# Positions of the global attention steps, and the order of the last output blocks, in a fused attention and two-MLP kernel

## Chip, cores and metric

The kernel runs on one core of one Trainium2 chip. The metric is the device time of one execution in microseconds (us); lower is better. The core's engines are PE (TensorE matmul; PEld is its weight load), DVE (VectorE), ACT (ScalarE), POOL (GpSimd) and SP (SyncE, which here only issues DMAs; SPq and ACTq are the DMA issues of SP and of ACT).

## What is computed

Attention over 32 global and 512 local positions (4 batches, 8 heads of 64), then two blocks on the 4 x 576 x 512 result, everything in float32:

```python
s_g = scale * q_g @ k_all.T                   # global rows see everything
out_g = sm(s_g) @ v_all
s_ll = where(|i - j| <= 32, scale * q_l @ k_l.T, -1e9)
s_l = concat([scale * q_l @ k_g.T, s_ll])     # local rows: a band and the globals
out_l = sm(s_l) @ concat([v_g, v_l])
x = concat([out_g, out_l]) as (4, 576, 512)
xn = (x - mean) / sqrt(var + 1e-6) * g_ln
x = x + relu(xn @ w_ch1) @ w_ch2              # first block, 512 -> 2048 -> 512
h = relu(x @ w_in)                            # second block, 512 -> 1024
conv = 3-tap convolution of h along the sequence
out = (h * sigmoid(conv)) @ w_out             # 1024 -> 512
```

## The kernel before

**Work units.** Most matmuls take a float32 operand as a high and a low part, so one product is three matmuls. Attention is cut into 64 local steps n = 0 to 63 (batch n // 16, tile t of 128 rows = n // 4 % 4, head pair hp = n % 4) and 16 global steps (one per batch and head pair). `GAT` (L37) says before which local step each global step stands; the list `order` is built from it. Rows of attention output are gathered into 17 tiles (16 local ones and one, "g", that holds all global rows), and the tiles into 8 chunks of 3, 2, 2, ... tiles. The first block (L825 hidden product, L849, L850 and L854 output product) runs chunk by chunk, in 16 units per chunk, while the attention of later chunks is mixed in: a pacing function (`tick`) hands out the small pieces of the steps so that, from a quarter of a chunk ahead of chunk k to a quarter ahead of chunk k + 1, the steps that chunk k + 1 needs are issued evenly (for k from 4 on, chunks counted from 0). A scheduler then fixes the order of each engine's instructions.

**Steps and their round trip.** A local step computes scores (L342, L343 on PE), adds the mask and takes the row limits (L346, DVE), and takes exponentials (L355, ACT). From n = 22 on the transposition of these goes through DRAM, for two steps (an even one and the odd one behind it, called pair 52/53 and so on) together: each step turns 32 x 32 blocks on DVE (L377) and stores them (`leave`, L381 on SP), and after the odd one four DMAs read both back in transposed order (`arrive`, L390 on SP). Then PE multiplies with the values, both steps behind each other (L416 for inner tiles, L409 to L411 for edge tiles t = 0 and 3). A global step has two halves of scores (L474, L475), a transpose on PE (L496) and its values (L505). L568 transposes a finished tile for the first block.

```python
for i, s in enumerate(order):
    s.out = i + 1
    if s.far and s.hp % 2:
        s.mate = [t for t in order[:i] if isinstance(t, Local)][-1]
        s.out = s.mate.out = i + LAG          # LAG = 3
```

So the values of a pair are issued three places in `order` behind its odd step, whatever stands in these places. SP issues its DMAs in order, among them the loads of later steps: `raw` (L298, L445, waits for POOL's split of the step whose buffer it takes), `rawv` (L303), `rawg` (L453), and the stores of finished tiles (`yscr`, L806).

**The end.** In the second block, `output(b, f)` (L1204) multiplies hidden block f of batch b with its 128 rows of `w_out`: for each of the four row tiles t three matmuls (L1192 to L1194) into that tile's own bank. Behind f = 7 each tile is copied to one of four buffers `osb` (`emit`, L1198) and stored. The rows of the 32 leading positions of all four batches lie together in `grem`, written by POOL (L1134, L1135), and make one product of 24 matmuls, `orem`. PE keeps program order in the whole second block. At the end come blocks 4, 5 and 6 of batch 3 (`steps[-4:-1]`), `orem` with four stores (L1252), then block 7 with the copies of its four tiles, by ACT and DVE in turn, the last tile in two halves of 256 columns (L1215, L1216).

Of the kernel before, what the change touches and what calls it, by code (L numbers as in the profile page):

```python
# [17 lines left out]
P = 128  # L18
B, H, SL, SG, D = 4, 8, 512, 32, 64
S = SL + SG  # L20
DM = H * D
FF, F2 = 2048, 1024
NF, NF2, NDC = FF // P, F2 // P, DM // P
NT = SL // P
# [9 lines left out]
BIG = 3.0e38  # L34

CHUNKS = [3, 2, 2, 2, 2, 2, 2, 2]
GAT = [24, 26, 28, 30, 32, 34, 36, 38, 40, 42, 44, 46, 49, 52, 53, 54]  # L37

WARM0 = 13
B_ATT = 300  # L40
# [32 lines left out]
def tile_kernel(ctx: ExitStack, tc: tile.TileContext, a_w, a_x, a_e, a_m, g_qk, g_v, w12, g_ln, w_in, w_out, conv_w, out):  # L73
    nc = tc.nc
    PE, DVE, ACT, POOL, SP = nc.tensor, nc.vector, nc.scalar, nc.gpsimd, nc.sync
# [24 lines left out]
    def keep_order(at, engines, to=None):  # L100

        last = {}
        for ins in traced()[at:to]:
            if ins.engine in engines:
                if ins.engine in last:
                    tc.add_manual_dep(ins, last[ins.engine].name, mybir.DependencyInfo(
                        mybir.DependencyClass.NoSync, mybir.DependencyReason.DATA), reason="order")
                last[ins.engine] = ins

    def copy(e, dst, src):  # L110
        if e is ACT:
            ACT.activation(dst, src, AF.Copy)  # L112
        else:
            e.tensor_copy(dst, src)

    def split(hi, lo, src, e_hi, e_lo):

        copy(e_hi, hi, src)
        return e_lo.tensor_tensor(lo, src, f32(hi), op=ALU.subtract)  # L119
# [25 lines left out]
    def w_stages(i, tag, fps, e_lo):  # L145

        n = 2 * DM // len(fps)
        cols = [slice(k * n, (k + 1) * n) for k in range(len(fps))]
        ops = []

        def start():
            raw = wraw.pop(i)
            for c, fp in zip(cols, fps):
                fp = fp()
                ops.append((fp, narrow(fp, raw[:, c], fp)))
                with behind("act"):
                    ops[-1][1][0]()

        def hi():
            w = wpool.tile([P, 2, 2 * DM], F32R, tag=f"w{tag}", name="w")  # L160
            wt[i] = w[:, 0], w[:, 1]
            for c, (fp, _) in zip(cols, ops):
                ACT.activation(w[:, 0, c], fp, AF.Copy)  # L163

        def lo():
            for c, (fp, _) in zip(cols, ops):
                e_lo.tensor_tensor(wt[i][1][:, c], fp, f32(wt[i][0][:, c]), op=ALU.subtract)

        def middle(k):
            for _, o in ops:  # L170
                o[k]()

        return [start], [lambda k=k: middle(k) for k in (1, 2)], [hi, lo]
# [80 lines left out]
    def next_qs(n):  # L254

        if n >= SPARE and spare:
            places[:] = spare
            spare.clear()
        places.append(places.pop(0))
        return places[-1]  # L260

    def score_bank(n):

        return (ps_t, "t") if n < SHARE else (ps_a, "s")
# [166 lines left out]
    class Global:  # L431
# [23 lines left out]
        def split(self):  # L455
            self.qs = next_qs(GAT[self.b * NP + self.hp])
            self.kh = apool.tile([P, S], F32R, tag="kh", name="kh", bufs=2)
# [8 lines left out]
        def half(self, i):  # L466
            ks = slice(i * self.HALF, (i + 1) * self.HALF)
            pool, tag = score_bank(GAT[self.b * NP + self.hp])
            ps = pool.tile([P, self.HALF], F32, tag=tag, name="ps")
# [57 lines left out]
    for n in range(B * NT * NP):  # L527
        b, t, hp = n // NP // NT, n // NP % NT, n % NP
        order += [Global(g // NP, g % NP) for g in range(B * NP) if GAT[g] == n]
        order.append(Local(b, t, hp, n))  # L530
        if hp == NP - 1:
            tiles.append((b, t))
            if n - NP < GAT[-1] <= n:
                tiles.append("g")
# [503 lines left out]
    for p in range(NPR):  # L1038
        st = w_stages(("o", p), p, [lambda k=k: mpool.tile([P, 2 * DM], F32, tag=f"fpx{k}", name="fpo")[:, :DM]
                                    for k in range(2)], DVE)  # L1040
# [68 lines left out]
    osbs = wpool.tile([P, 4, DM], F32, tag="w4", name="osb")  # L1109
    gts, ops = {}, {}  # L1110
# [27 lines left out]
    def hidden(b, p, at):  # L1138

        a, x = wae[p], wx[p]  # L1140
        n = b * NPR + p
        he, ho = hs[2 * n % 4], hs[(2 * n + 1) % 4]
        p1s, u2, u3 = (us[:, n % 2 * 3 + i] for i in range(3))

        def add(name, o, i0, i1):
            with ahead(B_ADD):
                named[name, n] = DVE.tensor_tensor(o, i0, i1, op=ALU.add)

        px = ps_x.tile([P, HB], F32, tag="px", name="px")
        product(px, a, 0, "B11", True, "first")  # L1150
        with ahead(B_ADD):
            named["p1s", n] = ACT.activation(p1s, px, AF.Copy)
        at("B11")
        py = ps_x.tile([P, HB], F32, tag="py", name="py")
        product(py, x, 1, "T2", True, "first")
        add("u2", u2, py, p1s)
        at("T2")
        pv = ps_v.tile([P, HB], F32, tag="pv", name="pv")
        product(pv, x, 0, "T3", True)
        add("u3", u3, pv, u2)  # L1160
        at("T3")
        pz = ps_v.tile([P, HB], F32, tag="pz", name="pz")
        product(pz, a, 2, "T1", True)
        add("e1", he[:, U1], pz, u3)
        at("T1")
        at(0)

        def t4():
            product(pv, a, 3, "T4", False)
            add("e0", he[:, U0], pv, u2)  # L1170
            named["relu", n] = ACT.activation(he[:, 1:1 + S], he[:, 1:1 + S], AF.Relu)
            at("T4")

        def b21():
            product(px, a, 1, "B21", False)
            with ahead(B_ADD):
                named["relu0", n] = ACT.activation(ho[:, U0], px, AF.Relu)
            at("B21")

        for part in (b21, t4) if n < 2 else (t4, b21):  # L1180
            part()
        gate(b, 2 * p, he)
        product(pz, x, 2, "B22", False)
        add("o1", ho[:, U1], pz, u2)
        named["relu1", n] = ACT.activation(ho[:, U1], ho[:, U1], AF.Relu)
        at("B22")
        gate(b, 2 * p + 1, ho)
        at(1)

    def mm_o(o, gh, gl, f, first, last):  # L1190
        wh, wl = (w[:, f % 2 * DM:(f % 2 + 1) * DM] for w in wt["o", f // 2])
        PE.matmul(o, gh, wh, start=first, stop=False)  # L1192
        PE.matmul(o, gh, wl, start=False, stop=False)  # L1193
        PE.matmul(o, gl, wh, start=False, stop=last)  # L1194

    nout = [0]

    def emit(o, e=ACT):  # L1198
        osb = osbs[:, nout[0] % 4]
        nout[0] += 1  # L1200
        copy(e, osb, o)
        return osb

    def output(b, f):  # L1204
        gh, gl = gts.pop((b, f))
        if f == 0:
            ops[b] = [ps_o.tile([P, DM], F32, tag=f"o{t}", name="po2") for t in range(NT)]
        for t in range(NT):
            tk = slice(SG + t * P, SG + (t + 1) * P)
            mm_o(ops[b][t], gh[:, tk], gl[:, tk], f, f == 0, f == NF2 - 1)  # L1210
            if (b, f, t) == (B - 1, NF2 - 1, NT - 1):
                osb = osbs[:, nout[0] % 4]
                for c, e, q in ((0, DVE, SP), (1, ACT, ACT)):
                    cols = slice(c * DM // 2, (c + 1) * DM // 2)
                    copy(e, osb[:, cols], ops[b][t][:, cols])  # L1215
                    q.dma_start(out[b, SG + t * P:SG + (t + 1) * P, cols], osb[:, cols])  # L1216
            elif f == NF2 - 1:
                e = DVE if b == B - 1 and t % 2 else ACT
                (ACT if e is DVE else SP).dma_start(out[b, SG + t * P:SG + (t + 1) * P, :], emit(ops[b][t], e))

    steps = [(b, f) for b in range(B) for f in range(NF2)]
    second = len(traced())
# [3 lines left out]
    for i in range(B * NPR):  # L1226
        b, p = divmod(i, NPR)
# [14 lines left out]
                    named["yc", b, n] = y_split(n)  # L1242

        hidden(b, p, at)
    for st in steps[-4:-1]:
        output(*st)
    o = ps_v.tile([P, DM], F32, tag="pv", name="orem")
    for f in range(NF2):
        mm_o(o, grem_h[:, f], grem_l[:, f], f, f == 0, f == NF2 - 1)
    orem = emit(o)  # L1250
    for b in range(B):
        (ACT if b % 2 else SP).dma_start(out[b, :SG, :], orem[b * SG:(b + 1) * SG])  # L1252
    output(*steps[-1])
    keep_order(second, [mybir.EngineType.PE])
    for order in HEAD + [[("e0", NPR * b + 2), ("sum", b, 3)] for b in range(1, B - 1)] + [
            [("u3", NPR * b + 3), ("e1", NPR * b + 3), e] for b in range(1, B - 1) for e in (("yc", b, "T3"), ("mul", b, 4))]:
# [113 lines left out]
```

## Time and profile before

| | us |
|---|---|
| median of 3 runs | 722.61 |
| lowest and highest of them | 719.81, 726.59 |
| the profiled execution | 721.07 |
| span of its trace | 719.3 |

The span is from the first to the last instruction of the profiled execution; the 1.77 us between it and that execution's own time lie outside the trace. A row of the timeline starts with its start in us from the span's start and its duration; what stands in brackets behind it is the idle time of that engine before it and what ended it. The matmuls of one row overlap, so PE's pace is read from the starts of successive rows.

### The profile page before, as it was taken

What the parts mean: (1) busy time and instruction counts of PE and PEld (TensorE: products, weight loads), DVE (VectorE), ACT (ScalarE), POOL (GpSimd) and SP (SyncE); (2) the same over time, 40 slices, a digit from 0 to 9 for tenths busy, and PEclk for the clock granted to TensorE, in tenths of its full rate; (3) what the DMA queues carried; (4) which work ended last, traced back from release to release, by engine and by line L of the source; (5) the groups of instructions that cost most, each with busy time, mean ns of one, the idle gap of its engine ahead of it and who ended that gap; (6) DMA issues with size and microseconds to landing.
All of it is one profiled execution on the core that took longest, in us unless ns stands there. A gap on an engine that the chain in (4) does not pass through costs nothing.

```text
span 719.3 us, 12803 instructions
## 1 busy us (share of the span) xinstructions
PE 703.3 (98%) x4517; PEld 627.9 (87%) x4517; DVE 474.6 (66%) x1168; ACT 402.5 (56%) x961; POOL 173.5 (24%) x236
## 2 busy tenths in 40 slices
PE   9989999999999999999989999999999999999997
PEld 5778899889988999999988999998899888988985
DVE  3889973755655475556538523763988989889770
ACT  6859663565566656656645411432656766566551
POOL 1012022444455344434434200000001122201000
PEclk9999999999999999999999999999999999999999
DMA  8993224775676667567547732315510121110102
GB/s 357 424 420 110 73 93 117 179 189 153 165 196 185 171 165 193 150 186 177 150 109 177 183 78 45 102 60 153 231 52 13 63 74 16 63 59 0 60 1 73
DMA packets 120144, 98.25 MB, mean 137 GB/s; under 512 B 84128, under 2 KB 102160, under 8 KB 117520
## 3 DMA queue, kind: packets, MB, share of 16 engines
q1 hardware_dynamic: 119552, 96.73, 46.2%
q8 instruction: 35, 0.57, 0.3%
q10 hardware_dynamic: 528, 0.70, 0.3%
q14 instruction: 29, 0.24, 0.1%
HBM read 77.49 MB, written 19.92 MB: 135 GB/s over the span
## 4 chain that ended last, share of the span: by engine, by line
PE 75%; DMA 11%; DVE 6%; ACT 2%; issue 2%; SPq 2%; POOL 0%; ACTq 0%; DVEq 0%; POOLq 0%
PE ph L825 20%; PE yps L854 7%; PE yps L849 7%; PE yps L850 6%; PE po L1194 4%; PE po L1193 4%; PE po L1192 4%; PE po L416 3%; DMA wraw<-w 3%; PE pv L1121 3%; PE px L1121 3%; PE pz L1121 3%; DMA trip<-trip 3%; DMA trip<-stage 3%; PE py L1121 1%
## 5 line engine op out<-in xcount | busy, mean ns | idle before, releaser
L825 PE MATMUL ph<-xe,w 128*128 128x256 f32 (+1 forms) x768 | 116.2, 297 | 0.9 <-ACT w L163 0.9
L825 PEld LDWEIGHTS ph<-xe,w 128*128 128x128 f32 x768 | 107.8, 188 | 5.8 <-ACT w L163 1.2
L849 PE MATMUL yps<-w,hh 128*128 128x512 f32 x272 | 109.4, 402 | 0.9 <-ACT hh L834 0.4
L850 PE MATMUL yps<-w,hh 128*128 128x512 f32 x272 | 107.7, 396 | 0.0
L825 PE MATMUL ph<-xo,w 128*128 128x256 f32 x768 | 105.5, 282 | 0.0
L834 ACT ACTIVATE hh<-ph 128x256 fp32r<-128x256 f32 (+1 forms) x128 | 50.4, 394 | 97.6 <-PE ph L825 86.0
L825 PEld LDWEIGHTS ph<-xo,w 128*128 128x128 f32 x768 | 99.9, 188 | 3.9
L119 POOL TENSOR_TENSOR kl<-raw,kh 128x448 fp32r<-128x448 f32 (+2 forms) x59 | 71.1, 1205 | 127.7 <-ACT kh L112 112.0
L835 DVE SCALAR_TENSOR_TENSOR hl<-ph,hh 128x256 fp32r<-128x256 f32 x112 | 46.4, 415 | 56.1 <-ACT hh L834 55.7
L854 PE MATMUL yps<-w,hl 128*128 128x512 f32 x224 | 72.5, 397 | 0.7 <-DVE hl L835 0.7
L346 DVE CUSTOM_DVE_ANT_0 sm<-ps,mask 128x192 f32<-128x192 f32 (+1 forms) x128 | 42.8, 368 | 33.9 <-PE ps L343 22.8
L355 ACT ACTIVATE sm<-sm,nm 128x192 f32<-128x192 f32 (+1 forms) x128 | 58.5, 458 | 10.1 <-DVE nm L346 9.8
L112 ACT ACTIVATE kh<-raw 128x448 fp32r<-128x448 f32 (+2 forms) x59 | 34.3, 581 | 48.1 <-PE ps L342 25.9
L849 PEld LDWEIGHTS yps<-w,hh 128*128 128x128 f32 x272 | 51.1, 188 | 8.9 <-ACT hh L834 1.4
L850 PEld LDWEIGHTS yps<-w,hh 128*128 128x128 f32 x272 | 51.2, 188 | 6.1
L1127 DVE SCALAR_TENSOR_TENSOR c<-hs,cw,c 128x544 f32<-128x544 f32 x64 | 48.9, 779 | 4.0 <-ACT c L1125 2.7
L1193 PE MATMUL po<-w,gh 128*128 128x512 f32 x128 | 50.7, 396 | 0.0
L1194 PE MATMUL po<-w,gl 128*128 128x512 f32 x128 | 50.7, 396 | 0.0
L854 PEld LDWEIGHTS yps<-w,hl 128*128 128x128 f32 x224 | 41.2, 188 | 10.8 <-DVE hl L835 1.9
L1192 PE MATMUL po<-w,gh 128*128 128x512 f32 x128 | 50.6, 395 | 0.0
L1134 POOL CAST grem<-gh 128x32 fp32r<-128x32 f32 x32 | 14.4, 450 | 120.3 <-ACT gh L112 120.3
L478 DVE CUSTOM_DVE_ANT_0 sm<-ps,tmpg 64x272 f32<-64x272 f32 x32 | 13.8, 431 | 37.2 <-ACT tmpg L477 37.2
(193 smaller groups left out, 1441.4 us busy)
## 6 DMA issues: line engine op xcount, KB each, us to landing
wraw<-w SPq DMA_DIRECT2D x16, 1024.0 KB, 17.1
trip<-trip SPq DMA_DIRECT2D x84, 128.0 KB, 3.3
raw<-a_m SPq DMA_DIRECT2D x23, 352.0 KB, 3.4
raw<-a_e SPq DMA_DIRECT2D x20, 320.0 KB, 3.3
trip<-trip SPq DMA_DIRECT2D x21, 256.0 KB, 3.7
trip<-stage SPq DMA_DIRECT2D x21, 256.0 KB, 3.2
raw<-g_qk SPq DMA_DIRECT2D x16, 304.0 KB, 3.0
rawg<-g_v SPq DMA_DIRECT2D x16, 280.0 KB, 3.5
```

The lines of the kernel that those rows point to most:

```text
L119: return e_lo.tensor_tensor(lo, src, f32(hi), op=ALU.subtract)
L355: ACT.activation(s, s, AF.Exp, bias=self.nm[:, j:j + 1], scale=-1.0, accum_out=xt.sums[:, h:h + 1])
L825: e = PE.matmul(ph[:, :n], w[:, d * P:(d + 1) * P], x[:, d], start=m == 0, stop=m == 3 * NDC - 1)
L834: ACT.activation(hh, ph[:, :n], AF.Relu)
L849: PE.matmul(yps[i], hh[:, tk], wh[:, DM:], start=edge(k, -1), stop=False)
L850: PE.matmul(yps[i], hh[:, tk], wl[:, DM:], start=False, stop=False)
L854: mark["last"] = PE.matmul(yps[i], hl[:, tk], wh[:, DM:], start=False, stop=edge(k, 1)).ins
L1121: PE.matmul(ps, wx_, y[:, d], start=start and d + m == 0, stop=d + m == 3, skip_group_check=True)
L1127: named[k, b, f] = DVE.scalar_tensor_tensor(c, h[:, k:S + k], cw[:, 3 * f + k:3 * f + k + 1], c, op0=ALU.mult, op1=ALU.add)
L1192: PE.matmul(o, gh, wh, start=first, stop=False)
L1193: PE.matmul(o, gh, wl, start=False, stop=False)
L1194: PE.matmul(o, gl, wh, start=False, stop=last)
```

## The change

It moves the global steps that stood in front of local steps 49, 52, 53 and 54 to stand in front of 48, 50, 52 and 54. At the end, `output` takes several hidden blocks at once: blocks 4 and 5 as before, then `orem` and its stores, then blocks 6 and 7 together, tile by tile (six matmuls for one tile, its copy, its store). All copies are ACT's; the last tile is copied whole and stored as two halves of 64 rows, one on SP's queue and one on ACT's.

```diff
-GAT = [24, 26, 28, 30, 32, 34, 36, 38, 40, 42, 44, 46, 49, 52, 53, 54]
+GAT = [24, 26, 28, 30, 32, 34, 36, 38, 40, 42, 44, 46, 48, 50, 52, 54]
...
-    def output(b, f):
-        gh, gl = gts.pop((b, f))
-        if f == 0:
+    def output(b, *fs):
+        pairs = [gts.pop((b, f)) for f in fs]
+        if fs[0] == 0:
             ops[b] = [ps_o.tile([P, DM], F32, tag=f"o{t}", name="po2") for t in range(NT)]
         for t in range(NT):
             tk = slice(SG + t * P, SG + (t + 1) * P)
-            mm_o(ops[b][t], gh[:, tk], gl[:, tk], f, f == 0, f == NF2 - 1)
-            if (b, f, t) == (B - 1, NF2 - 1, NT - 1):
-                osb = osbs[:, nout[0] % 4]
-                for c, e, q in ((0, DVE, SP), (1, ACT, ACT)):
-                    cols = slice(c * DM // 2, (c + 1) * DM // 2)
-                    copy(e, osb[:, cols], ops[b][t][:, cols])
-                    q.dma_start(out[b, SG + t * P:SG + (t + 1) * P, cols], osb[:, cols])
-            elif f == NF2 - 1:
-                e = DVE if b == B - 1 and t % 2 else ACT
-                (ACT if e is DVE else SP).dma_start(out[b, SG + t * P:SG + (t + 1) * P, :], emit(ops[b][t], e))
+            for f, (gh, gl) in zip(fs, pairs):
+                mm_o(ops[b][t], gh[:, tk], gl[:, tk], f, f == 0, f == NF2 - 1)
+            if fs[-1] == NF2 - 1:
+                rows, osb = out[b, tk], emit(ops[b][t])
+                if (b, t) == (B - 1, NT - 1):
+                    ACT.dma_start(rows[D:], osb[D:])
+                    rows, osb = rows[:D], osb[:D]
+                SP.dma_start(rows, osb)
...
-    for st in steps[-4:-1]:
+    for st in steps[-4:-2]:
         output(*st)
...
-    output(*steps[-1])
+    output(B - 1, NF2 - 2, NF2 - 1)
```

PE's order around the values of pair 52/53 (L416, the `x8`), before. L505 and L496 are a global step's, L474 and L475 its scores, L849 to L854 and L825 the first block's:

```order
L854 MATMUL yps<-w,hl 128x512 x2
L505 MATMUL pog<-v,ptsb 128x256 x5
L568 MATMUL ptx<-ident,xn 128x128 x4
L849 MATMUL yps<-w,hh 128x512
L850 MATMUL yps<-w,hh 128x512
L849 MATMUL yps<-w,hh 128x512
L850 MATMUL yps<-w,hh 128x512
L854 MATMUL yps<-w,hl 128x512 x2
L416 MATMUL po<-rawv,trip 128x64 x8
L474 MATMUL ps<-kh,xe 128x272
L475 MATMUL ps<-kl,xe 128x272
L825 MATMUL ph<-xe,w 128x256 x24
```

And the same values in the changed kernel, with the scores of steps 54 (first) and 55 (L342, L343):

```order
L342 MATMUL ps<-kh,xe 128x224
L343 MATMUL ps<-kl,xe 128x224
L342 MATMUL ps<-kh,xe 128x224
L343 MATMUL ps<-kl,xe 128x224
L825 MATMUL ph<-xe,w 128x256 x12
L416 MATMUL po<-rawv,trip 128x64 x5
L496 MATMUL ptg<-ident,sm 109x128 x5
L342 MATMUL ps<-kh,xe 128x224
L343 MATMUL ps<-kl,xe 128x224
L342 MATMUL ps<-kh,xe 128x224
L343 MATMUL ps<-kl,xe 128x224
L416 MATMUL po<-rawv,trip 128x64 x3
```

Before, the values stood ahead of the second half of the last global step (L474) and of the scores of step 54; now they stand behind step 54's scores and 12 more matmuls of L825.

ACT's last instructions, before (`po_8022` to `po_8025` are the banks of tiles 0 to 3 of batch 3; `DMA` is an issue on ACT's queue):

```order
L112 ACTIVATE osb<-orem 128x512
L112 ACTIVATE osb<-po_8022 128x512
L1252 DMA out<-osb 32x512 x2
L1219 DMA out<-osb 128x512
L112 ACTIVATE osb<-po_8024 128x512
L112 ACTIVATE osb<-po_8025 128x256
L1216 DMA out<-osb 128x256
```

And in the changed kernel:

```order
L112 ACTIVATE osb<-orem 128x512
L1250 DMA out<-osb 32x512 x2
L112 ACTIVATE osb<-po_8022 128x512
L112 ACTIVATE osb<-po_8023 128x512
L112 ACTIVATE osb<-po_8024 128x512
L112 ACTIVATE osb<-po_8025 128x512
L1215 DMA out<-osb 64x512
```

ACT now copies all four tiles whole, and its queue holds only two stores of `orem` and the lower half of the last tile.

SP's last issues, before:

```order
L1004 DMA yT<-yscr 128x4x544
L1219 DMA out<-osb 128x512 x8
L1252 DMA out<-osb 32x512 x2
L1219 DMA out<-osb 128x512
L1216 DMA out<-osb 128x256
L1219 DMA out<-osb 128x512
```

And in the changed kernel:

```order
L1004 DMA yT<-yscr 128x4x544
L1217 DMA out<-osb 128x512 x8
L1250 DMA out<-osb 32x512 x2
L1217 DMA out<-osb 128x512 x3
L1217 DMA out<-osb 64x512
```

Before, tile 2's store (the last row) stood behind the store of tile 3's first half; now the tiles' stores stand in their order, and the last is half a tile.

## Rows read from the trace of the kernel before

**Rows 1.** Page, part 1: engine, busy us (share of span), instructions.

```profile
PE 703.3 (98%) x4517; PEld 627.9 (87%) x4517; DVE 474.6 (66%) x1168; ACT 402.5 (56%) x961; POOL 173.5 (24%) x236
```

**Rows 2.** Windows: stretch, its length, then busy us (instructions) of PE, PEld, DVE, ACT, POOL; clock, DMA share, GB/s.

```profile
200.00:250.00 50.00, 48.12 (x332) 43.75 (x331) 28.32 (x103) 32.76 (x92) 25.56 (x25) 1.00 0.69 179
...
350.00:400.00 50.00, 47.31 (x329) 43.27 (x328) 30.43 (x99) 27.73 (x80) 20.97 (x22) 1.00 0.57 142
...
694.00:719.30 25.30, 20.26 (x91) 16.25 (x89) 7.50 (x11) 7.34 (x13) 1.28 (x4) 0.94 0.15 52
```

**Rows 3.** Waits of PE from 60 to 425 us: total us, times, longest.

```profile
PE po L416 <- DMA trip<-trip: 3.1, 3, 2.2
PE po L409 <- DMA trip<-trip: 1.3, 1, 1.3
```

**Rows 4.** Timeline of PE, 355 to 395 us: scores of 53, its values; scores of 55, its values.

```profile
356.58 0.37 PE L342 MATMUL ps<-kh,xe 128*128 128x224 f32 x1
...
365.52 0.63 PE L854 MATMUL yps<-w,hl 128*128 128x512 f32 x2
368.30 2.08 PE L416 MATMUL po<-rawv,trip 128*128 128x64 f32 x16 [2.15 <-DMA trip<-trip]
...
377.17 0.27 PE L342 MATMUL ps<-kh,xe 128*128 128x224 f32 x1
...
390.08 0.66 PE L416 MATMUL po<-rawv,trip 128*128 128x64 f32 x4 [0.52 <-DMA trip<-trip]
```

**Rows 5.** Timeline of SP: `leave` of 53, `arrive` of 52/53.

```profile
359.92 0.38 SPq L381 DMA_DIRECT2D trip<-stage  x1
363.56 1.92 SPq L390 DMA_DIRECT2D trip<-trip  x4
```

**Rows 6.** Chain that ended last, one piece of L825: start, us, what.

```profile
370.69 2.84 PE ph L825 x24
```

**Rows 7.** Timeline of PE: scores of 33 and values of 32/33; scores of 43 and values of 42/43.

```profile
198.75 0.25 PE L342 MATMUL ps<-kh,xe 128*128 128x192 f32 x1
...
211.79 0.50 PE L409 MATMUL po<-rawv,trip 128*128 128x128 f32 x2 [1.29 <-DMA trip<-trip]
...
273.88 0.35 PE L342 MATMUL ps<-kh,xe 128*128 128x224 f32 x1
...
286.29 1.76 PE L416 MATMUL po<-rawv,trip 128*128 128x64 f32 x14
```

**Rows 8.** Timeline of the end, all engines.

```profile
701.74 0.21 POOL L1135 CAST grem<-gl 128x32 fp32r<-128x32 f32 x1
...
703.06 0.39 PE L1192 MATMUL po<-w,gh 128*128 128x512 f32 x1
...
711.07 0.40 PE L1194 MATMUL orem<-w,grem 128*128 128x512 f32 x1
...
711.51 0.60 ACT L112 ACTIVATE osb<-orem 128x512 f32<-128x512 f32 x1 [10.70 <-PE orem L1194]
...
713.87 0.39 PE L1194 MATMUL po<-w,gl 128*128 128x512 f32 x1
...
714.70 0.42 DVE L114 COPY osb<-po 128x256 f32<-128x256 f32 x1 [1.10 <-ACT osb L112]
...
715.16 0.38 ACT L112 ACTIVATE osb<-po 128x256 f32<-128x256 f32 x1 [0.47 <-DVE osb L114]
715.57 0.38 ACTq L1216 DMA_DIRECT2D out<-osb  x1
715.61 0.37 SPq L1219 DMA_DIRECT2D out<-osb  x1
```

**Rows 9.** DMA issues from 714 us on: out<-in queue, count, KB each, median us to landing.

```profile
out<-osb SPq DMA_DIRECT2D x1, 256.0 KB, 2.7
out<-osb SPq DMA_DIRECT2D x1, 128.0 KB, 1.7
out<-osb ACTq DMA_DIRECT2D x1, 128.0 KB, 1.9
```

More of the change, by code (lines that the diff above doesn't have):

```diff
@@ L1196, in tile_kernel, with emit @@
     nout = [0]
-    def emit(o, e=ACT):
+    def emit(o):
         osb = osbs[:, nout[0] % 4]
         nout[0] += 1
-        copy(e, osb, o)
+        copy(ACT, osb, o)
         return osb
-    def output(b, f):
-        gh, gl = gts.pop((b, f))
-        if f == 0:
+    def output(b, *fs):
+        pairs = [gts.pop((b, f)) for f in fs]
+        if fs[0] == 0:
             ops[b] = [ps_o.tile([P, DM], F32, tag=f"o{t}", name="po2") for t in range(NT)]
```

## Prediction

> **What bounds the kernel now.** I read the page's busy times first, then windows, then PE's waits, then the timelines around them. PE is busy for 703.3 of 719.3 us [rows 1], and the change leaves the number of its matmuls as it is. So only PE's idle time (16 us in all) and what follows its last matmul can give anything. The windows say where to look: 200 to 250 us leaves PE 1.9 us idle, 350 to 400 us 2.7 us, and the end, 694 to 719.3 us, 5.0 us [rows 2]. The first of these lies ahead of everything that the change moves: PE's order differs only from local step 48 on, about 310 us into the trace. The list of waits names the cause in the middle: from 60 to 425 us PE waited 3.1 us in three times on L416 and 1.3 us once on L409, each time for the round trip of a pair's exponentials through DRAM [rows 3]. Two of these lie in reach: 2.15 us ahead of the values of pair 52/53 and 0.52 us ahead of those of 54/55, together 2.67 us [rows 4].
>
> **Why pair 52/53 waits.** Two lengths race. One is the round trip from the odd step's scores until its data are back. For 53 it is 368.30 - 356.58 = 11.7 us [rows 4], of which 3.3 pass until SP issues `leave`, 3.6 more until the first `arrive`, and the rest in the four DMAs of `arrive` [rows 5]. The other is the PE work queued between these scores and the pair's values: the last matmul ahead of the wait ends at 365.52 + 0.63 = 366.15, so 9.6 us. For 55 it is 12.9 us of round trip against 12.4 of work, for 33 it is 13.0 against 11.8 (edge values, L409), and 43 had 12.4 us of work and did not wait [rows 4, 7]. I counted the same distance for all 21 pairs in PE's order, at 0.118 us for a matmul of L825 [rows 6], 0.233 us for one with 512 columns (twelve from 711.07 to 713.87, [rows 8]) and about 0.25 us for a value matmul (a listed one is two records; 16 records take 2.08 us, [rows 4]). Three pairs come out below 11 us (22/23, 32/33 and 52/53), and all three waited; 18 have 12.0 us or more, and only 54/55 waited. So the line lies between 11 and 12 us.
>
> **Part 1, the global steps.** It removes the gap's cause: before, a global step stood between 52 and 53 and the next one right behind 53, and the values of 52/53 came ahead of step 54's scores; now two local steps lie side by side and the values come behind step 54's scores. Between 53's scores and the values stand 48 matmuls of L825 instead of 24, with 18 of 512 columns in both: 24 x 0.118 = 2.8 us more, so about 12.0 us by count and 12.3 by the trace's 9.6. The other pairs behind the point where the orders part: 46/47 12.2 us, 50/51 12.0, 54/55 12.4, 48/49 14.6, the four last over 18. None is below 11 us. 22/23 and 32/33 lie ahead of that point and keep their 0.4 and 1.3 us.
> What is late next: with a round trip of c us, the four shortest distances wait (c - 12.2) + 2 (c - 12.0) + (c - 12.4) in all. At 11.7 us, as 53 itself had, that is nothing; at 12.9, as 55 had, 3.0 us. I take 0.3 us: one of the 18 pairs of that length waited, for 0.52, which over nine moved pairs is 0.26. Both ends, 0 and 3.0, stay for the range. Nothing is added to the steps themselves: the same loads, stores and round trips pass through SP's queue. Two things there are new: for 50/51 a `raw` load stands between `leave` and `arrive`, which costs nothing while its issue is over within the 3.6 us that `arrive` waits anyway [rows 5]; and the stretch that prepares chunk 5 holds 12 steps instead of 11, the next one 6 instead of 7. DVE, ACT and POOL, busy for about 30, 28 and 21 of 50 us there [rows 2], cover that. Net: -2.67 + 0.3 = -2.4 us.
>
> **Part 2, the end.** The order of blocks costs PE nothing: `orem` moves ahead of block 6's 12 matmuls, so it begins at 703.06 instead of 2.8 us later, and the last cast of `grem` is over at 701.74 + 0.21 = 701.95 [rows 8]. Block 7's operands are older than that cast. The cover is 1.1 us, and if it were gone PE would wait for the difference.
> What counts is the tail behind the last matmul, which ends at 713.87 + 0.39 = 714.26 [rows 8]; the span ends at 719.3, 5.0 us later. Before, four copies fall due within three matmuls (0.7 us) of each other; the first half of the last tile starts on DVE at 714.70, the second on ACT at 715.16, because each waited for the other engine, and tile 2's store leaves SP at 715.61 behind the first half's. That store of 256 KB lands 2.7 us later [rows 9], at 718.3, and the span ends 1.0 us behind it. After, a tile is due every six matmuls, 1.4 us, and a copy takes 0.60, so the last copy starts at once: 714.26 + 0.04 (as `orem`'s copy behind 711.47) + 0.60 + 0.03 to the issue (715.54 to 715.57) = 714.93 [rows 8]. Tile 2's store left 1.4 us earlier and is out of the way. The landing of the last two halves of 128 KB is not in the trace. Halves of the same size, cut by columns, took 1.7 and 1.9 us, a whole tile 2.7 [rows 9]; both halves together are a whole tile issued on two queues, so I take 2.2, between 1.7 and 2.7. With 1.0 us behind it the end is 718.1: 1.2 us gained, bounds 0.7 and 1.7.
> The rows show halves by columns, issued 0.4 us apart, and none by rows. The Trainium skill ("DMA: Bandwidth & Descriptors", Rules for kernel authors) speaks against this cut: "Two transfers to disjoint partition halves: Don't bother — they serialize", since both spread over the same 16 engines. By that rule the pair lands like one whole tile, and the gain would be the lower bound.
>
> **Sum.** -2.4 - 1.2 = -3.6 us on the profiled execution's 721.07: 717.5. That execution lies 1.54 us below the median of the three runs (722.61); the forecast is for a median, so I start in the middle of the two, 721.84, and arrive at 718.3. In per cent this is half of one; 1% is 7.2 us, about as much as the three runs differ among themselves (6.8 us) and about what a measurement of this kernel can tell from no change.
>
> **Rivals**, each from 721.84:
> - *The wait moves on.* Distances of 12.0 to 12.4 us turn out too short, with a round trip of 12.9 us as pair 54/55 had it: -2.67 + 3.0 - 1.2 = -0.9, 721.0. For it: 54/55 waited at 12.4. Against it: 17 pairs of that length or more did not.
> - *The two halves land like one whole tile.* Landing 2.7 us: -2.4 - 0.7 = -3.1, 718.8. For it: the whole tile's 2.7 us; against it: the halves' 1.7 and 1.9, which overlapped. It is the skill's rule, worked out from rows 9.
> - *Slower: the denser stretch lengthens the round trips.* Place: the four pairs at 12.0 to 12.4 us, where 12 steps share DMA engines that are busy for 0.57 to 0.69 of the time [rows 2], with a 352 KB load between `leave` and `arrive` of 50/51. It decides from c = 13.1 us, where the new waits (4 c - 48.6) exceed 2.67 + 1.2. At 14 us they are 7.4, so +3.5: 725.3. For it: 13.0 us was seen (33). Against it: nothing in the trace reached 13.1, and 12 steps to a chunk is what the earlier chunks hold too.
>
> **Chances and range.** Forecast 0.55, halves like one tile 0.20, wait moves on 0.15, slower 0.10. The likely cases lie between -4.3 (both bounds at their best) and -0.9, that is 717.5 to 721.0; a median of so scattered runs adds some 2 us on either side, so 715.5 to 723.0, which leaves the slower case out. Faster by over 1% would need 7.2 us, more than all terms at their best, and comes from scatter alone: 0.04. Slower by over 1% is the upper half of the slower case and scatter: 0.04. Within 1%: 0.92.
>
> **What would show it.** Right: no wait of PE above 0.3 us for the round trip between 310 and 425 us, in place of 2.15 and 0.52; PE's last matmul about 2.4 us earlier than 713.87; ACT's last copy within 0.1 us of it, at 128x512; the span's end 3.7 to 4.0 us behind that matmul. Wrong: waits for `trip` at the values of 46/47, 50/51, 52/53 or 54/55; a gap ahead of `orem`; a last landing over 2.7 us.

## The result, and the profile after

| | before | after |
|---|---|---|
| median, us | 722.61 | 716.51 |
| lowest and highest, us | 719.81, 726.59 | 714.89, 717.97 |
| executions | 11 | 11 |
| the profiled execution | 721.07 | 715.16 |
| span of its trace | 719.3 | 713.4 |

The ratio of the medians is 0.9912, with a 95% interval of 0.9891 to 0.9932: 6.1 us less, where 3.6 were forecast from a starting point of 721.84. The two traces differ by 5.9 us.

Page, part 1, of the kernel after:

```profile
PE 701.4 (98%) x4517; PEld 627.9 (88%) x4517; DVE 471.6 (66%) x1166; ACT 402.8 (56%) x962; POOL 173.6 (24%) x236
```

PE does the same 4517 matmuls as in [rows 1]; its idle time has gone from 16.0 to 12.0 us. PE's waits for the round trip, 60 to 425 us, which answer to [rows 3]:

```profile
PE po L409 <- DMA trip<-trip: 0.9, 1, 0.9
...
PE po L416 <- DMA trip<-trip: 0.4, 1, 0.4
```

The 2.2 us of L416 are gone. What is left are pairs 32/33 (0.9) and 22/23 (0.4), both ahead of the place where the change begins. The windows that answer to [rows 2], with one more for the stretch that the change reaches (length, then PE, PEld, DVE, ACT, POOL; clock, DMA share, GB/s):

```profile
200.00:250.00 50.00, 48.63 (x335) 44.40 (x334) 28.61 (x104) 32.60 (x92) 25.47 (x25) 1.00 0.70 182
310.00:425.00 115.00, 114.91 (x800) 106.26 (x799) 64.29 (x213) 57.69 (x172) 40.54 (x43) 1.00 0.65 156
350.00:400.00 50.00, 50.00 (x356) 46.64 (x355) 34.20 (x111) 29.45 (x89) 22.09 (x24) 1.00 0.72 181
694.00:713.40 19.40, 15.15 (x66) 12.01 (x64) 2.40 (x4) 4.52 (x8) 1.27 (x4) 0.96 0.21 68
```

From 350 to 400 us PE was idle for 2.7 us and is now idle for none; over the whole 115 us it is idle for 0.1. In the last window PE is busy for 15.15 us, that is from 694 without a gap until its last matmul ends (708.76 + 0.40 = 709.16, 5.1 us earlier than before). So `orem` found its operands ready.

PE's timeline at the pairs of [rows 4]: scores of 53, first part of the values of 52/53, scores of 55, values of 54/55:

```profile
353.48 0.27 PE L342 MATMUL ps<-kh,xe 128*128 128x224 f32 x1
...
365.33 1.29 PE L416 MATMUL po<-rawv,trip 128*128 128x64 f32 x10
...
366.95 0.35 PE L342 MATMUL ps<-kh,xe 128*128 128x224 f32 x1
...
379.46 1.52 PE L416 MATMUL po<-rawv,trip 128*128 128x64 f32 x12
```

No bracket stands behind either row of L416: 365.33 - 353.48 = 11.9 us of work lay ahead of the values of 52/53 (9.6 before), and 12.5 ahead of those of 54/55, and neither waited.

The end, which answers to [rows 8]: copies on ACT, the last matmul, the issues of the last tile (SP's row holds four stores, the last of them the tile's upper half), and the landings from 708 us on ([rows 9]):

```profile
707.80 0.60 ACT L112 ACTIVATE osb<-po 128x512 f32<-128x512 f32 x1 [0.79 <-PE po L1194]
...
708.76 0.40 PE L1194 MATMUL po<-w,gl 128*128 128x512 f32 x1
709.19 0.60 ACT L112 ACTIVATE osb<-po 128x512 f32<-128x512 f32 x1 [0.79 <-PE po L1194]
...
705.84 4.52 SPq L1217 DMA_DIRECT2D out<-osb  x4
709.82 0.56 ACTq L1215 DMA_DIRECT2D out<-osb  x1
```

```profile
out<-osb SPq DMA_DIRECT2D x1, 256.0 KB, 2.1
out<-osb SPq DMA_DIRECT2D x1, 128.0 KB, 2.3
out<-osb ACTq DMA_DIRECT2D x1, 128.0 KB, 2.7
```

The last copy starts 0.03 us behind the last matmul, as the prediction had it. Its halves then take 2.3 and 2.7 us to land, not 2.2: from PE's last matmul to the end are 4.2 us (5.0 before), so the tail gave 0.8 us, not 1.2.

Where the 5.9 us between the traces lie: the ends of the chunks (L857, the last additions of a chunk, on DVE) cut both traces in the same places. Chunk 3 ends at 322.79 before and at 322.17 after. The same cut at the ends of chunks 5, 6 and 7 and at the last matmul gives these windows, before:

```profile
322.79:444.35 121.56, 118.87 (x822) 109.51 (x821) 61.68 (x201) 53.80 (x158) 35.57 (x38) 1.00 0.55 135
444.35:489.65 45.30, 45.30 (x293) 41.05 (x292) 28.64 (x59) 16.01 (x32) 0.55 (x1) 1.00 0.25 70
...
535.30:714.26 178.96, 178.91 (x1069) 159.38 (x1067) 142.90 (x246) 106.29 (x196) 24.52 (x64) 1.00 0.13 42
```

And after:

```profile
322.17:440.10 117.93, 117.84 (x817) 108.89 (x816) 61.56 (x200) 52.84 (x157) 35.14 (x38) 1.00 0.59 143
440.10:485.40 45.30, 45.30 (x293) 41.04 (x292) 28.67 (x59) 16.11 (x32) 0.55 (x1) 1.00 0.25 70
...
530.63:709.15 178.52, 178.52 (x1069) 159.45 (x1067) 142.16 (x245) 107.25 (x197) 24.77 (x64) 1.00 0.14 45
```

Of 5.9 us, 0.6 lie ahead of the change, 3.6 in its stretch (2.6 of them PE's idle time, 2.69 us before and 0.09 after; the rest is 1.0 us of busy time over five records fewer, and half of that is no gain of this stretch: the five records are one group of L496, some 0.5 us, which lies behind the first cut before, at 324.25, and ahead of it after, at 319.00), 0.4 between 489.65 and 535.30, 0.4 in the second block, 0.8 in the tail. PE's clock is 1.00 in all these windows, in both traces. So a pair of single traces gives -3.6 and -0.8 us for the two parts, and the rest is how these two executions differ. The medians differ by nearly as much, 6.1 us, but part of that has a reason that neither of these two traces holds; the experiments found it.

### The profile page after: what moved, and what is told of

Its sections match the earlier page's. It is cut to its first block, busy times and chain, and to the rows that moved or that the text cites. A ratio compares the mean times of both kernels' runs of the same rounds, so it can differ in the third digit from the quotient of the medians.

```text
span 713.4 us, 12797 instructions
## 1 busy us (share of the span) xinstructions
PE 701.4 (98%) x4517; PEld 627.9 (88%) x4517; DVE 471.6 (66%) x1166; ACT 402.8 (56%) x962; POOL 173.6 (24%) x236
## 4 chain that ended last, share of the span: by engine, by line
PE 83%; DMA 9%; DVE 3%; SPq 2%; issue 1%; ACT 1%; POOL 0%; DVEq 0%; ACTq 0%; POOLq 0%
PE ph L825 23%; PE yps L849 8%; PE yps L854 8%; PE yps L850 8%; DMA wraw<-w 6%; PE po L1194 4%; PE po L1193 4%; PE po L1192 4%; PE pz L1121 3%; PE pv L1121 3%; PE px L1121 3%; PE po L416 3%; PE py L1121 2%; PE ps L342 1%; DMA yscr<-x 1%
## 5 line engine op out<-in xcount | busy, mean ns | idle before, releaser
L825 PE MATMUL ph<-xe,w 128*128 128x256 f32 (+1 forms) x768 | 116.1, 297 | 0.9 <-ACT w L163 0.9
L825 PEld LDWEIGHTS ph<-xe,w 128*128 128x128 f32 x768 | 107.6, 188 | 5.6 <-ACT w L163 1.2
L849 PE MATMUL yps<-w,hh 128*128 128x512 f32 x272 | 109.0, 401 | 0.9 <-ACT hh L834 0.4
L825 PE MATMUL ph<-xo,w 128*128 128x256 f32 x768 | 106.9, 283 | 0.0
L825 PEld LDWEIGHTS ph<-xo,w 128*128 128x128 f32 x768 | 100.2, 188 | 3.8
L854 PE MATMUL yps<-w,hl 128*128 128x512 f32 x224 | 72.3, 396 | 0.5 <-DVE hl L835 0.5
L346 DVE CUSTOM_DVE_ANT_0 sm<-ps,mask 128x192 f32<-128x192 f32 (+1 forms) x128 | 42.5, 368 | 34.3 <-PE ps L343 23.4
L849 PEld LDWEIGHTS yps<-w,hh 128*128 128x128 f32 x272 | 51.1, 188 | 8.9 <-ACT hh L834 1.4
L854 PEld LDWEIGHTS yps<-w,hl 128*128 128x128 f32 x224 | 41.0, 188 | 9.9 <-DVE hl L835 1.2
L552 POOL TENSOR_TENSOR small<-small 128x1 f32<-128x1 f32 x17 | 11.6, 683 | 106.7 <-DVE small L551 106.7
```

The lines of the kernel that those rows point to most:

```text
L825: e = PE.matmul(ph[:, :n], w[:, d * P:(d + 1) * P], x[:, d], start=m == 0, stop=m == 3 * NDC - 1)
L849: PE.matmul(yps[i], hh[:, tk], wh[:, DM:], start=edge(k, -1), stop=False)
L854: mark["last"] = PE.matmul(yps[i], hl[:, tk], wh[:, DM:], start=False, stop=edge(k, 1)).ins
```

## The experiments

In the expectations of the first four runs, Theory A and Theory B stand for what each of them says itself. From *The kernel before, profiled again* on, Theory A is that a wait of PE lowers its granted clock for a while in many executions, and Theory B that a wait costs its idle time alone.

**Each part alone.** The kernel before with the new positions:

```diff
-GAT = [24, 26, 28, 30, 32, 34, 36, 38, 40, 42, 44, 46, 49, 52, 53, 54]
+GAT = [24, 26, 28, 30, 32, 34, 36, 38, 40, 42, 44, 46, 48, 50, 52, 54]
```

> The moved global steps alone, the end as before. Theory A (the round-trip waits of 52/53 and 54/55 are most of the gain, and a wait costs its idle time plus about 0.16 us of matmul overlap that the row hides): no wait for trip between 310 and 425 us, the stretch from the end of chunk 3's output product (x, L857, near 322 us) to that of chunk 5's (near 444 us before) shorter by about 3.6 us, the median 3.5 to 4.5 us below before's. Theory B (the end is worth as much as the waits): 2.0 to 3.0 us below.

Measured: 718.49 us (six executions, 717.57 to 719.52) against 723.37 for the kernel before on the same chip, ratio 0.993 (0.9914 to 0.9946): 4.9 us. The tail is 5.0 us, as before, and PE waits for no round trip between 310 and 425 us. The stretch between the ends of chunks 3 and 5 takes 441.16 - 323.12 = 118.0 us, 3.5 less than in the first trace of before, as expected; but the median fell by more than the 3.5 to 4.5 us of its Theory A.

The changed kernel with the old positions:

```diff
-GAT = [24, 26, 28, 30, 32, 34, 36, 38, 40, 42, 44, 46, 48, 50, 52, 54]
+GAT = [24, 26, 28, 30, 32, 34, 36, 38, 40, 42, 44, 46, 49, 52, 53, 54]
```

> The new end alone, the global steps as before. Theory A: the waits of 2.15 and 0.52 us are still there, the tail behind PE's last matmul is about 4.2 us instead of 5.0, the median 0.8 to 1.5 us below before's. Theory B: 2.5 to 4 us below, by more than the shorter tail shows.

Measured: 722.05 us (twelve executions, 719.19 to 724.27), ratio 0.9982 (0.9963 to 1.0001): 1.3 us, with an interval that just includes no change. The tail in its trace is 4.2 us. The two parts add up, 0.70 + 0.18 = 0.88%, which is the whole change. So the end is not far from the 1.2 us of the forecast, and the steps give 4.9 us where 2.4 were forecast. This trace also shows what follows the wait ahead of 52/53's values, in its windows:

```profile
366.00:370.00 4.00, 1.77 (x10) 1.27 (x9) 1.32 (x4) 1.82 (x5) 1.54 (x1) 0.93 0.54 96
370.00:374.00 4.00, 4.00 (x20) 4.00 (x20) 0.06 (x1) 0.95 (x3) 0.29 (x1) 0.50 0.20 51
374.00:378.00 4.00, 4.00 (x27) 3.96 (x26) 1.40 (x7) 1.85 (x6) 1.58 (x2) 0.72 0.37 109
378.00:382.00 4.00, 4.00 (x30) 3.69 (x29) 2.57 (x9) 2.79 (x9) 1.89 (x2) 1.00 0.26 58
```

PE was idle for 2.2 of the first four microseconds. Then it is busy without a gap, but at a granted clock of 0.50, the 1.2 GHz level, and gets through 20 matmuls in four microseconds; in the last row, at 1.00, it gets through 30 (their shapes differ). This is the term that the forecast lacks.

**One wait put back.** The changed kernel with one of its global steps within pair 52/53:

```diff
-GAT = [24, 26, 28, 30, 32, 34, 36, 38, 40, 42, 44, 46, 48, 50, 52, 54]
+GAT = [24, 26, 28, 30, 32, 34, 36, 38, 40, 42, 44, 46, 48, 50, 53, 54]
```

> The changed kernel with one global step put back inside pair 52/53 (in front of 53 instead of 52). PE's order then holds about 8.9 us of work between 53's scores and the values of 52/53. Theory A: a wait of 2 to 3 us for trip at these values and nowhere else, the median 2 to 3.5 us above the changed kernel's 716.5, so 718.5 to 720. Rival (it is the even spacing of all steps over the stretches that pays, not the short distance): within 1 us of the changed kernel.

Measured: 720.66 us (eleven executions, 718.80 to 723.37), ratio 0.996 (0.9945 to 0.9974), so 4.1 us over the changed kernel's median, or 3.5 by the two ratios to the kernel before (0.996 and 0.9912). The one is above the 2 to 3.5 us expected, the other at their upper end; the rival, by which it would be within 1 us, is out. The wait is there, and so is the fall behind it:

```profile
PE po L416 <- DMA trip<-trip: 2.2, 1, 2.2
```

```profile
362.00:366.00 4.00, 1.79 (x9) 1.70 (x9) 0.44 (x2) 1.02 (x3) 1.43 (x1) 0.76 0.35 53
366.00:370.00 4.00, 4.00 (x20) 4.00 (x20) 0.65 (x3) 1.17 (x3) 0.94 (x1) 0.50 0.23 66
370.00:374.00 4.00, 4.00 (x28) 3.78 (x27) 1.73 (x9) 2.88 (x10) 2.10 (x3) 0.88 0.33 94
```

A wait of 2.2 us costs 3.5 to 4.1: it is this one wait, in this one place, that makes most of the difference between the two kernels.

**One store for the last tile.** The changed kernel with the last tile stored whole on SP's queue:

```diff
-                if (b, t) == (B - 1, NT - 1):
-                    ACT.dma_start(rows[D:], osb[D:])
-                    rows, osb = rows[:D], osb[:D]
```

> The changed kernel with the last tile stored by one DMA of 128 rows on SP's queue instead of two halves on two queues. If the two halves run side by side, the last landing takes longer by 0.3 to 0.6 us than the changed kernel's 2.7; if they share the engines and the split only adds a second completion, the one store lands in 2.1 to 2.7 us, and the tail is the same or up to 0.5 us shorter. The median moves by less than 1 us either way.

Measured: 716.67 us (six executions, 712.95 to 719.63), ratio 0.9898 (0.987 to 0.9926). The interval does not set it apart from the changed kernel's 0.9912. Its three executions with a mean clock of 0.999 or 1.0 took 712.95 to 716.15 us, the three with 0.995 to 0.997 717.19 to 719.63, so here too the clock varies. But the trace shows the piece by itself: the tail is 3.5 us instead of 4.2, and its three tile stores from 705 us on read

```profile
out<-osb SPq DMA_DIRECT2D x3, 256.0 KB, 2.0
```

One whole tile of 256 KB lands in 2.0 us; its two halves took 2.3 and 2.7. So the cut costs 0.7 us; the 2.0 is even less than the 2.1 to 2.7 expected for halves that share the engines. The rule of the Trainium skill that the prediction weighed ("DMA: Bandwidth & Descriptors", Rules for kernel authors: halves by partitions serialize) agrees with this.

**The kernel before, profiled again.** No edit.

> The kernel before, unchanged, profiled once more. Theory A (a wait of PE of some 2 us is followed, in many executions, by a fall of the granted clock): the wait ahead of 52/53's values is again near 2.2 us, and in the 10 us behind it windows of 4 us show a granted clock well under 1 (0.5 to 0.9), with the chunk end behind it some 3 us later than in the first profile (385.9). Theory B (a wait costs its idle time alone): the same wait, the clock 1.00 behind it, chunk ends as in the first profile within 1 us.

Measured: 726.82 us in this one execution, span 725.0. The waits are those of [rows 3] (3.0 us on L416, longest 2.3; 1.3 us on L409). What follows each of them is not the same. Windows behind 32/33 (first two rows) and around 52/53 (the others):

```profile
206.00:212.00 6.00, 4.48 (x25) 3.61 (x24) 3.60 (x17) 5.10 (x15) 3.87 (x5) 0.99 0.70 142
212.00:218.00 6.00, 6.00 (x29) 6.00 (x29) 1.69 (x8) 2.49 (x9) 2.11 (x3) 0.50 0.67 181
...
370.00:374.00 4.00, 2.77 (x17) 2.80 (x18) 0.00 (x0) 0.00 (x0) 0.00 (x0) 0.78 0.15 36
374.00:378.00 4.00, 4.00 (x20) 4.00 (x20) 1.03 (x4) 1.97 (x5) 1.87 (x2) 0.50 0.29 62
378.00:382.00 4.00, 4.00 (x26) 3.74 (x25) 2.05 (x10) 2.51 (x9) 1.27 (x2) 0.86 0.16 63
```

The trace of before from which the forecast was made, in the same stretch behind 32/33 and behind 52/53:

```profile
212.00:218.00 6.00, 5.94 (x49) 5.70 (x49) 3.13 (x11) 4.41 (x13) 3.00 (x3) 1.00 0.77 210
...
366.00:370.00 4.00, 1.85 (x16) 1.73 (x15) 1.04 (x3) 1.08 (x3) 1.04 (x1) 1.00 0.36 63
370.00:374.00 4.00, 4.00 (x35) 4.00 (x35) 1.37 (x6) 2.72 (x8) 1.89 (x2) 1.00 0.35 91
```

The same waits of the same kernel, once with the clock at 1.00 behind them and once at 0.50. The same 24 matmuls of L825, two matmuls behind the values of 52/53, take in the trace with the fall

```profile
374.40 5.11 PE L825 MATMUL ph<-xe,w 128*128 128x256 f32 x24
```

and in the first trace

```profile
370.53 3.00 PE L825 MATMUL ph<-xe,w 128*128 128x256 f32 x24
```

The window between the ends of chunks 3 and 5 gives the price. In the trace with the fall it is

```profile
325.35:450.47 125.12, 122.09 (x822) 112.61 (x821) 61.68 (x200) 53.79 (x158) 35.75 (x38) 0.97 0.54 131
```

and took 121.56 us, 118.87 of them busy, in the first trace of before (shown with the result). With the same 822 matmuls PE is busy for 3.2 us more, and idle for 0.3 us more. So the fall behind this one wait costs 3.2 us, more than the wait itself (2.3). Chunk 4 ends 6.0 us later than in the first trace (391.87 against 385.89), not some 3 us, because 2.6 us were already lost at the end of chunk 3, behind the fall at 32/33.

**The wait filled with work.** The kernel before, positions and end untouched, with eight matmuls of the identity by itself in the bank that the values of 52 overwrite afterwards:

```diff
+    dep = mybir.DependencyInfo(mybir.DependencyClass.NoSync, mybir.DependencyReason.DATA)
+    def fill(po, k=8):
+        p, at = [t for t in traced() if t.engine == mybir.EngineType.PE][-12], len(traced())
+        [PE.matmul(po, ident, ident, start=True, stop=True) for _ in range(k)]
+        [tc.add_manual_dep(t, p.name, dep, reason="order") for t in traced()[at:]]
...
+            self.n == 52 and fill(po)
```

> The kernel before (old positions, old end), with 8 idle-filling matmuls of 128 x 128 on the identity written into the bank of 52's values before these; they keep PE busy where it waited, and the values of 52/53 and 54/55 come 13 us of PE work or more behind their odd steps' scores. The 2.7 us of waiting are gone and 2.0 to 2.6 us of added work stand in their place. Theory A (idle time lowers the clock for several us): the mean clock is 0.997 or more in nearly all executions and the median is 2 to 3 us below the kernel before, ratio 0.996 to 0.997. Theory B (a wait costs its idle time alone): no change, ratio 0.999 to 1.001.

Measured: 720.97 us (twelve executions, 719.33 to 723.20) against 723.66, ratio 0.9966 (0.9948 to 0.9985). Its trace:

```profile
366.09 0.36 PE L474 MATMUL ps<-kh,xe 128*128 128x272 f32 x1 [1.04 <-DVE nm L478]
...
377.35 1.73 PE L121 MATMUL po<-ident 128*128 128x128 f32 x14
378.92 1.30 PE L416 MATMUL po<-rawv,trip 128*128 128x64 f32 x10
```

The values of 52/53 no longer wait, but not for the added work alone: in the order that came of the edit they also stand behind the scores of 54 and 55, 23.5 us behind those of 53 (355.47). The added work takes about 2.0 us, and a wait of 1.0 us has come up at a global step (L474). In idle and added time that is about as much as the 2.7 us it replaces, and by the ends of its chunks the stretch takes 443.12 - 321.33 = 121.8 us, as in the first trace of before (121.6). Yet the median is 2.7 us lower. In the trace the clock is 1.00 in every window from 350 to 394 us; the mean granted clock of a whole execution was 0.997 or more in 8 of these 12 executions, and in 3 of the 29 of the kernel before on the same chip. The 8 took 719.33 to 721.42 us, the 3 took 720.22 to 721.87: at an equal clock the two kernels are alike. (The expectation had nearly all executions at 0.997 or more.) With as much useless work in place of the waiting the kernel is faster, so it is what the waiting does to the clock that costs; Theory B, by which nothing should have changed, is out.

**A larger dose.** The changed kernel with global steps within pairs 44/45 and 52/53, and also within 40/41 and 48/49:

```diff
-GAT = [24, 26, 28, 30, 32, 34, 36, 38, 40, 42, 44, 46, 48, 50, 52, 54]
+GAT = [24, 26, 28, 30, 32, 34, 36, 38, 41, 44, 45, 46, 49, 52, 53, 54]
```

> The changed kernel with its new end, but global steps in front of 45 and 53 (within two pairs): distances 9.3 us for 44/45 and 10.1 for 52/53, where PE then waits 2 to 3 us at the one and 1.6 to 2.8 at the other. Theory A (idle time and a lower clock behind it in many executions, as one such pair cost 4.1 us): 8 to 10 us above the changed kernel, ratio to the kernel before 1.002 to 1.005, with windows of clock 0.5 to 0.8 behind both waits. Theory B (idle time alone): 4.5 to 5 us above the changed kernel, ratio 0.997 to 0.999.

Measured: 726.15 us (ten executions, 724.20 to 729.75), ratio 1.0043 (1.0023 to 1.0063), 9.6 us over the changed kernel: Theory A's size. But the trace does not have the waits where they were expected. There are four of over 1 us, 1.9 us at 283 us (L416, pair 42/43), 1.4 at 310 (L409, pair 44/45), 1.9 at 340 (L342, for DVE) and 1.5 at 377 (L849, for ACT), and none ahead of 52/53's values. The clock falls behind the first and the third; behind the first:

```profile
282.00:284.00 2.00, 0.92 (x5) 0.95 (x6) 0.87 (x4) 0.91 (x5) 1.52 (x2) 0.81 0.67 194
284.00:286.00 2.00, 2.00 (x11) 2.00 (x11) 0.00 (x0) 0.00 (x0) 0.00 (x0) 0.50 0.03 8
286.00:288.00 2.00, 2.00 (x11) 1.90 (x10) 0.82 (x2) 0.44 (x1) 0.00 (x0) 0.50 0.75 217
288.00:290.00 2.00, 2.00 (x6) 1.61 (x5) 1.90 (x4) 0.00 (x0) 0.00 (x0) 0.50 0.59 199
290.00:292.00 2.00, 2.00 (x17) 1.86 (x17) 0.16 (x2) 0.00 (x0) 0.55 (x1) 0.98 0.00 1
```

The total does not decide for A, though. PE's idle time in this trace is 727.9 - 708.0 = 19.9 us, 7.9 more than in the changed kernel's (12.0), where Theory B had reckoned with 4.5 to 5; and the execution with the highest mean clock, 0.998, still took 724.20 us. Most of the 9.6 us can be idle time, so the run does not separate the theories, as it was meant to. It shows something else, in the scores of 43 and the values of 42/43:

```profile
268.08 0.27 PE L342 MATMUL ps<-kh,xe 128*128 128x224 f32 x1
...
283.08 2.23 PE L416 MATMUL po<-rawv,trip 128*128 128x64 f32 x10 [1.87 <-DMA trip<-trip]
```

This pair had 13.1 us of work ahead of its values, more than the line of 11 to 12 us, and waited all the same: the round trip took 15.0 us, longer than any in the trace of before.

**Fewer waits still.** Three versions, all with the whole last store, take the wait at 32/33 away too, by having no global step in front of 32. The first puts one in front of 22 instead:

```diff
-GAT = [24, 26, 28, 30, 32, 34, 36, 38, 40, 42, 44, 46, 48, 50, 52, 54]
+GAT = [22, 24, 26, 28, 30, 34, 36, 38, 40, 42, 44, 46, 48, 50, 52, 54]
```

> The changed kernel with global steps in front of 22 and of every even step but 32 up to 54, and the last tile stored whole on SP's queue. 32/33's distance goes from 10.8 to 14.7 us of PE work, 22/23's from 10.9 to 10.5. Theory A: the wait at 32/33 (0.9 to 1.4 us) is gone with the fall of the clock that sometimes follows it, 22/23's grows by 0.4; with the whole store's 0.7 the median is 1.5 to 2.2 us under the changed kernel, ratio to the kernel before 0.988 to 0.989. Theory B (only the idle time counts): 0.5 less waiting and 0.7 less tail, 1.2 us under the changed kernel, ratio 0.9895. If the wait moves to 22/23 in full (2 us), nothing beyond the store: 0.990.

Measured: 724.42 us, ratio 1.001 (0.9994 to 1.0025). The wait at 32/33 is gone, but the values of the first global step are now loaded into a buffer (L451) that still serves as the low part of the first chunk's hidden values (L830), so that part of the first chunk's output product, or of that global step's, is computed from the other's data. This version does not compute the same result, so its time tells nothing of the waits. PE stands still there:

```profile
PE pog L505 <- POOL v L119: 5.2, 1, 5.2
```

The second and the third leave 22 free and put two global steps in front of 54, or in front of 28:

```diff
+GAT = [24, 26, 28, 30, 34, 36, 38, 40, 42, 44, 46, 48, 50, 52, 54, 54]
...
+GAT = [24, 26, 28, 28, 30, 34, 36, 38, 40, 42, 44, 46, 48, 50, 52, 54]
```

> The changed kernel with the last tile stored whole on SP's queue, and the global step of 32 moved to the end: two stand in front of 54. Distances: 32/33 goes from 10.8 to 14.9 us of PE work, 52/53 to 11.6, 58/59 to 12.1, 22/23 stays at 10.9, the others 12.0 or more. Theory A (idle time and, in a part of the executions, several us of a lower clock behind it): 32/33's wait of 0.8 to 1.4 us and what follows it are gone, 1.5 to 2.5 us under the kernel with the whole store alone (ratio 0.9898), ratio 0.9865 to 0.988. Theory B (idle time alone): 0.9 us, ratio 0.9885. If 11.6 us is too short for 52/53, its wait takes the place of 32/33's: ratio 0.989 to 0.991.

Measured: 722.63 us (twelve executions, 718.81 to 726.21), ratio 1.0002 (0.9975 to 1.0029), a miss. No pair waits for long (0.6 us at most), but where the two global steps stand together, the scores of one (L474) wait 1.7 us for DVE's row limits of a local step (L346), and behind that the clock falls:

```profile
350.00:354.00 4.00, 2.29 (x19) 2.09 (x19) 3.34 (x14) 3.54 (x12) 3.54 (x4) 1.00 0.70 211
354.00:358.00 4.00, 4.00 (x24) 4.00 (x23) 3.88 (x7) 1.79 (x6) 2.68 (x3) 0.60 0.66 210
```

The five executions with a mean clock of 0.997 or more took 718.8 to 720.8 us, the seven with 0.995 or less 722.3 to 726.2: one kernel, 5 us apart, the slower part at the lower clock. The clock is not all of the miss: PE's idle time in this trace is 717.8 - 703.6 = 14.2 us, 3.6 more than with the whole store alone (711.2 - 700.6 = 10.6).

> As the run before, but two global steps in front of 28 instead of 54, none in front of 32. Distances: 32/33 16.2 us, 30/31 11.9, 36/37 and 42/43 11.8, 22/23 10.9, the others 12.0 or more. Theory A: ratio 0.9865 to 0.988 if 11.8 is enough; Theory B: 0.9885. If 11.8 is too short, two or three small waits of 0.2 to 1 us: ratio 0.989 to 0.991.

Measured: 714.97 us (five executions, 713.35 to 715.30), ratio 0.9885 (0.9861 to 0.9909), the lowest of all, under both kernels; from the version with the whole store alone (0.9898) its interval does not set it apart. The wait at 32/33 is gone; 1.0 us ahead of 22/23's values, 0.45 ahead of one pair more and 0.8 at a local step's scores (L342, for DVE's row limits of a global step) are left. All five executions ran at a mean clock of 0.999 or 1.0, so nothing here tells A from B.

## Why the prediction was right, and where its size was off

- **Where the time is, and which waits go: right.** The forecast was faster by half a per cent and within 1%; it is 0.88%, inside the range, but 716.51 lies under the likely cases (717.5 to 721.0) and is in the range only by the 2 us added for scatter: that part is luck. (The lowest case adds up to -4.4, not -4.3; its 717.5 stays.) The waits ahead of 52/53 and 54/55 went, nothing waits between 310 and 425 us, and 11.9 us of work between 53's scores and the values were enough. The line between 11 and 12 us is less sharp than it was put. It mixes two measures: 32/33 has under 11 us by count and 11.8 by the trace, and it waited, here too (0.9). And the round trip varies: 15.0 us in *A larger dose*, where 13.1 us of work were not enough.
- **"What is late next": right.** I took 0.3 us for new waits; there are none. The rivals *the wait moves on* and *slower* did not come about: no pair behind the point where the orders part waits, and the `raw` load ahead of 50/51's `arrive` cost nothing.
- **The step that was mis-sized is the first term of "Net: -2.67 + 0.3 = -2.4 us".** It priced a wait at PE's idle time in one execution. The runs show that what follows costs as much again: the steps alone gave 4.9 us, one such wait put back cost 3.5 to 4.1, and with the wait replaced by useless work the median fell by 2.7 although PE did nothing useful sooner. The profiled execution of before happened to have no fall of the clock (1.00 in all its windows from 322 us to PE's last matmul), so its trace could not show the term. PE's last matmul ended 5.1 us earlier than in that trace, not 2.4; some 1.5 of these lie outside the stretch of the moved steps and were not explained. The term could be seen only in how the executions of before scatter, 719.8 to 726.6 us, which the forecast took for a scatter of the measurement and put into the range.
- **The starting point failed for the same reason.** 721.84 is the middle of the profiled execution and the median, that is between executions without the fall and executions with it. On the chip of the first four experiments, 3 of 21 executions of before had a mean clock of 0.997 or more, at a median of 720.0 us; 16 had 0.995 or less, at 723.7. The changed kernel's 11 executions all had 0.997 to 1.0, at a median of 716.5. From 720.0 that is 3.5 us, near the forecast's sum of 3.6; the other 2.6 of the 6.1 are then the clock. The comparison is across chips, so only its size counts.
- **Part 2, the end: the copy right, the landing mis-sized.** The order of blocks cost PE nothing, the last copy starts at once. The term of 2.2 us for the halves' landing measured 2.3 and 2.7, so the tail gave 0.8 instead of 1.2 us, and the end lies 4.2 us behind the last matmul, outside the 3.7 to 4.0 named as a sign. The rival *two halves land like one whole tile* had it right, and even lenient: one whole store behind a free queue lands in 2.0.
- **Not settled:** which waits the clock falls behind. In these traces (the first of *Fewer waits still* left out) it fell behind waits of 1.3, 1.4, 1.4, 1.7, 1.9, 1.9, 2.2, 2.2 and 2.3 us, and did not behind 0.9, 1.0, 1.0, 1.1, 1.3, 1.4, 1.5, 1.7 and 2.2: longer ones more often, but length alone does not decide. And of the 1.0 us of busy time between the two first traces, half was not taken apart.

## What to carry to other kernels

Where PE is busy for 98% of the span, price a wait of about two microseconds at more than its idle time: here 2.2 us cost 3.5 to 4.1 in the median, and 2.3 + 3.2 in an execution with the fall. Look at the granted clock of the windows behind it in more than one execution before trusting one trace. When executions of a kernel scatter by a per cent, compare their mean clocks first: the scatter may be a term that the change removes. A distance in work between a producer and its consumer, counted from the order of one engine, forecast the waits of the changed kernel, but it is worth no more than the round trip that it is held against: with more steps moved, a pair with 13.1 us waited.

## What the runs showed of the hardware

The granted clock goes to 0.50, the 1.2 GHz level, for 3 to 7 us behind waits of PE as short as 1.3 us, in a part of the executions of one and the same program: 29 matmuls in six microseconds behind 32/33 in one execution of before, 49 in the other. The price came in two sizes: what the clock lacks to 1.00, summed over windows of 2 us, is about 1.7 us in four of the nine falls and 3.4 us in five (in *A larger dose* 0.38 + 1.00 + 1.00 + 1.00 + 0.04); where PE's busy time could be compared, the latter cost 3.2 us. In the matmul counts the fall is as plain as in the clock column, so it is no artefact of that column. The Trainium skill ("TensorE: Matmul & The Clock Gate", HAM oscillation) tells of a kernel that falls back to the low level behind each wait for a DMA. The rows here agree that waits do this, behind 1.3 to 2.3 us of waiting, seven times for a round trip through DRAM and twice for DVE, in some executions and not in others.
